# One PSUM tile of two banks made into two tiles of one bank, in a kernel of gated linear attention and a mixture of experts

## The chip, the cores and the metric

The kernel runs on one core of one Trainium2 chip. The metric is the device time of one execution in microseconds; the time of a kernel is the median of its runs. A core has a matrix engine (TensorE, PE in the rows; its weight loads are PEld), a vector engine (VectorE, DVE), a scalar engine (ScalarE, ACT), GpSimd (POOL), and SyncE (SP), which issues transfers here. The matrix engine writes into PSUM, an accumulator memory of eight banks in this program's layout, and the other engines read it from there.

## The reference

First a linear attention with a decay for each channel, over 4 batches of 8 heads, 768 steps and 48 channels a head. Its result is laid out as 3072 rows of 384 numbers. Then a mixture of 8 experts: every row is given to an expert by a greedy choice over all scores in falling order, at most 384 rows an expert, and each expert is a feed-forward network with 1024 hidden units.

```python
for t in range(S):
    state = alpha[:, :, t, :, None] * state + np.einsum('bhd,bhe->bhde', k[:, :, t], v[:, :, t])
    y[:, :, t] = np.einsum('bhd,bhde->bhe', q[:, :, t], state)
...
logits = x @ w_gate
order = np.argsort(-logits.flatten())
for idx in order:
    tok, e = (int(idx) // E, int(idx) % E)
    if assigned[tok] >= 0 or counts[e] >= cap:
        continue
    assigned[tok] = e
    counts[e] += 1
...
h = np.maximum(x[mask] @ w1[e], 0.0)
out[mask] = h @ w2[e]
```

## The kernel before

**The attention** works on 24 units: 6 chunks of 128 steps for each of the 4 batches, all 8 heads of a unit together, four pairs of two. For each unit VectorE makes running products of the decay (lines 449 and 454) and scales keys (`kh`, line 459), GpSimd scales queries (`qh`, line 464), TensorE multiplies them into scores (line 495), eight products of 128 by 128 that alternate between the two heads of a pair, and ScalarE moves the scores from PSUM to the tile `sm` (line 500), one half for each head. GpSimd masks each half (line 502), TensorE multiplies with the values (line 541), and ScalarE stores the result in `yta` (line 564).

The scores lie in the PSUM tile `s`: `[128, 2, HP, C]` with `HP` = 4 and `C` = 128, in 4-byte numbers, so two banks, one for each head of the pairs.

**The hand-over.** When the last unit is done, its router scores (lines 574 to 591) are sorted out on VectorE. Line 655 compares the keys of the last four units with the limits of the first digit, line 676 counts on TensorE, line 683 finds the threshold `gg` on VectorE, lines 901 and 902 spread it on TensorE, line 949 makes the next key `nd`, line 920 compares it with the next digit's limits, line 891 counts again, and line 895 makes the next `gg`. Further digits follow in the same manner (lines 867 to 884), then the row indices of the first expert's rows (line 1106), and GpSimd gathers these rows from `x_dram` (line 1110).

Before a row can be gathered, the attention result must lie in `x_dram` with a row's numbers next to each other. For this the result of each unit, a chunk, is turned by TensorE, four transposes a chunk in two steps of two (line 692), evicted by ScalarE into `xga` (line 696) and stored by SyncE (line 701). The first six chunks are turned in the score tile `s`, even ones in its first bank and odd ones in its second:

```python
for n in range(Y_IN_ATTENTION):
    o = sps[:, n % 2].rearrange("p a b -> p (a b)")
    xo = None
    for h in range(2):
        xo = op("PE", 0.2, shape=128, fn=lambda n=n, h=h, o=o: (turn_out(n, o, 2 * h), turn_out(n, o, 2 * h + 1)),
                r=[("yt", n)], after=[*lastw["sm", NU - 1], *([xo] if h else [])], banks=(f"S{n % 2}",), at=40.0 + n,
                take=None if h else f"s{n % 2}")
```

The other 18 are turned in the tiles `turned`, which take over the banks of `d`, `s` and `y` when the attention's pool is closed. Fills (line 291, on a tile of zeros, into `d`) stand between them on TensorE.

**The order of the work.** A planner inside the kernel (`plan`) puts the operations of all engines in an order, by durations, banks and due times that are written in the code. There are two plans, one for the attention with the six turned chunks, and one for the rest, from the routing on. The planner's own idea of the banks, the names `S0` and `S1`, keeps the two halves of the score tile apart. The order goes to a framework that adds the waits between engines. It follows tiles: an instruction waits for the earlier readers and writers of the same tile. It also has a say where the two plans meet on an engine.

Of the kernel before, what the change touches and what calls it, by code (L numbers as in the profile page):

```python
# [8 lines left out]
F32 = mybir.dt.float32  # L9
# [28 lines left out]
AF = mybir.ActivationFunctionType  # L38
# [4 lines left out]
def gla_moe_kernel(ctx, tc, q, k, v, alpha, w_gate, w12, out):  # L43
    nc = tc.nc
    C = 128
    NC = 6
    H = 8
    HP = H // 2
# [10 lines left out]
    warm = consts.tile([128, 512], BF)  # L59
# [92 lines left out]
    ps = att.enter_context(tc.tile_pool(name="ps", bufs=1, space=bass.MemoryType.PSUM))  # L152
# [24 lines left out]
    RXG = RING["xg"]  # L177

    dps = ps.tile([128, 2, 512], F32, name="d").rearrange("p a b -> p (a b)")
    sps = ps.tile([128, 2, HP, C], F32, name="s")  # L180
    yps = ps.tile([128, 2, 512], F32, name="y")
    yvs = [z[:, :, :2 * C].rearrange("p h (s t) -> p h s t", t=C) for z in (yps, dps.rearrange("p (a b) -> p a b", a=2))]
    xx = psa.tile([128, 2, 512], F32, name="xx")
# [16 lines left out]
    def op(eng, dur, fn, r=(), w=(), banks=(), at=0.0, after=(), lat=LAT, take=None, give=None, follow=(), boost=0.0,  # L200
           dma=0.0, soft=(), small=False, shape=None, ahead=0.12,
           clear=None, until=None, again=LAT):
        o = Op()
        o.small, o.shape, o.ahead, o.clear, o.until, o.again = small, shape, ahead, clear, until, again
        o.take, o.give, o.follow, o.boost, o.dma, o.soft = take, give, follow, boost, dma, soft
        o.eng, o.dur, o.fn, o.banks, o.at, o.lat = eng, dur, fn, banks, at, lat
        o.idx = len(ops)
        pre = set(after)
        for key in r:
            pre |= set(lastw[key])  # L210
            users.setdefault(key, []).append(o)
        for key in w:
            nm, ver = key
            old = (nm, ver - RING.get(nm, 1))
            pre |= set(users.get(old, ())) | set(lastw.get(old, ()))
            lastw.setdefault(key, []).append(o)
        o.pre = pre
        ops.append(o)
        return o
# [64 lines left out]
    V, G, A, P_ = nc.vector, nc.gpsimd, nc.scalar, nc.tensor  # L284
# [16 lines left out]

    def spin(n):
        for _ in range(n):
            P_.matmul(sps[:, 0].rearrange("p a b -> p (a b)"), warm[:, :128], warm, start=True, stop=True)

    def dinit():
        V.memset(dps[:, :904], 0.0)
# [2 lines left out]
    c_d = op("DVE", 1.2, dinit, w=[("dinit", 0)])  # L310
    c_pad = op("ACT", 1.9, pads, w=[("pads", 0)], banks=("Y", "KX"))
    op("PE", 4.0, lambda: spin(WARM_UP), banks=("S0",))

    def wgate():
# [120 lines left out]
    def unit(n):  # L435
        c, b = divmod(n, NBAT)
        a, sc, ga = AL[n % RING["al"]], SC[n % RING["sc"]], GA[n % RING["ga"]]
        kh, qh, kn = KH[n % RING["kh"]], QH[n % RING["qh"]], KN[n % RING["kn"]]
        sm, ms, st_ = SM[n % RING["sm"]], MS[n % RING["m"]], ST[b]
# [5 lines left out]
        for i, (lo, hi) in enumerate(parts):  # L445
            f = len(parts)
# [27 lines left out]
            if p1 > pm:  # L474
# [4 lines left out]
               r=[("q", n), ("ga", n)] + ([("kh", n)] if n in K_FIRST else []), w=[("qh", n)], at=n + 0.1)  # L479
# [11 lines left out]
        def scores():  # L491
            for p in range(HP):
                for h in range(2):
                    hs = slice(64 * h, 64 * h + 64)
                    P_.matmul(sps[:, h, p], kh[hs, p], qh[hs, p], start=True, stop=True)  # L495

        op("PE", 0.9, scores, shape=64, r=[("kh", n), ("qh", n)], w=[("S0", n), ("S1", n)], banks=("S0", "S1"),
           at=n + 0.3 - (AHEAD_S if n >= NU - 2 else 0.0))
        for h in range(2):
            op("ACT", 0.6, lambda h=h: A.activation(sm[:, h], sps[:, h], AF.Copy), r=[(f"S{h}", n)],  # L500
               w=[("sm", n)], banks=(f"S{h}",), at=n + 0.4)
            op("POOL", 0.65, lambda h=h: G.affine_select(  # L502
                sm[:, h], sm[:, h], pattern=[[0, HP], [1, C]], compare_op=OP.is_ge, fill=0.0, base=0,
                channel_multiplier=-1), r=[("sm", n)], w=[("sm", n)], at=n + 0.5)
# [12 lines left out]
        if c:  # L517
            if n in M_ACT:
                for p in range(HP):
                    op("ACT", 0.226, lambda p=p: A.activation(ms[:, p], st_[:, p], AF.Copy, scale=total[:, p:p + 1]),  # L520
                       r=[("sc", n), ("st", n - NBAT)], w=[("m", n)], at=n + 0.15)
            else:
                op("POOL", 0.5, lambda: G.tensor_tensor(ms, st_, bc(total, D), op=OP.mult),
                   r=[("sc", n), ("st", n - NBAT)], w=[("m", n)], at=n + 0.15)
# [166 lines left out]
    def turn_out(n, o, j):  # L691
        P_.transpose(o[:, C * j:C * j + KO], YT[n][:KO, j % 2, j // 2], ident[:KO, :KO])  # L692

    def y_evict(n, o):
        b, c = n % NBAT, n // NBAT
        A.activation(XG[c % RXG][:, b].rearrange("p (j g d) -> p j g d", g=2, d=D),
                     o.rearrange("p (j g d) -> p j g d", j=4, g=2)[:, :, :, :D], AF.Copy)

    def y_store(n, m=1):
        b, c = n % NBAT, n // NBAT  # L700
        nc.sync.dma_start(x_dram.rearrange("(b c p) d -> c p b d", b=NBAT, c=NC)[c][:, b:b + m],
                          XG[c % RXG][:, b:b + m])

    for n in range(NU):
        loads(n)
        unit(n)
        if n == 2:
            for i, (e, d_, f) in enumerate(rows):
                lates.append(op(e, d_, f, after=[*lates[-1:], *lastw["qh", n]], at=CONST_AT + CONST_STEP * i))
        for g, (n0, n1) in enumerate(LOGITS):  # L710
            if n1 == n + 1:
                logits(g, range(n0, n1))
        if n == GROUPS[0][1] - 1:
            first_copied = copied[-1]
# [1 line left out]
    choice(1, *GROUPS[1], copied[-1])  # L716
    ev = []
    for n in range(Y_IN_ATTENTION):
        o = sps[:, n % 2].rearrange("p a b -> p (a b)")
        xo = None  # L720
        for h in range(2):
            xo = op("PE", 0.2, shape=128, fn=lambda n=n, h=h, o=o: (turn_out(n, o, 2 * h), turn_out(n, o, 2 * h + 1)),
                    r=[("yt", n)], after=[*lastw["sm", NU - 1], *([xo] if h else [])], banks=(f"S{n % 2}",), at=40.0 + n,
                    take=None if h else f"s{n % 2}")
        ev.append(op("ACT", 0.5, lambda n=n, o=o: y_evict(n, o), after=[xo], banks=(f"S{n % 2}",), at=40.0 + n,
                     give=f"s{n % 2}"))
        op("SP", 0.1, lambda n=n: y_store(n), after=ev[-1:], at=40.0 + n)
# [674 lines left out]
```

## Time and profile before

| | us |
|---|---|
| median of 3 runs | 377.22 |
| lowest and highest run | 377.16, 380.49 |
| the profiled execution | 376.25 |
| its span, first to last instruction | 374.70 |
| TensorE busy | 354.2 |
| VectorE busy | 268.6 |
| ScalarE busy | 186.5 |
| GpSimd busy | 179.5 |

The profile records one execution, with a row for each instruction. Times in rows count from the start of the span. TensorE overlaps its products, so a busy TensorE is not one at its peak. The attention fills the span up to about 99 us, the routing of the first expert's rows goes to about 125, and the feed-forward part takes the rest, with the routing of later experts beside it.

### The profile page before, as it was taken

The page shows a single profiled execution, that of the slowest core. Times are in us where ns is not written, and L with a number is a line of the kernel's source. Part 1 is how long each engine was busy: PE and PEld are TensorE (multiplying, and loading weights), DVE is VectorE, ACT ScalarE, POOL GpSimd, SP SyncE. Part 2 cuts the span into 40 slices and gives each one's busy share as a digit, 9 for nine tenths or more (in the row PEclk, how much of TensorE's full clock was granted, in tenths as well). Part 3 has the DMA queues.
Part 4 walks back from the last instruction along what each step waited for, and adds up shares of the span by engine and source line. Part 5 has one row for each costly group of instructions (what it writes and reads, how often), then busy time and mean ns, then how long its engine had stood idle before and what let it go on. Part 6 is the DMA issues. An engine that isn't in the chain of part 4 may idle for free.

```text
span 374.7 us, 9683 instructions
## 1 busy us (share of the span) xinstructions
PE 354.2 (95%) x3716; PEld 313.3 (84%) x3716; DVE 268.6 (72%) x741; ACT 186.5 (50%) x387; POOL 179.5 (48%) x298
## 2 busy tenths in 40 slices
PE   8999999999898899999999999999999999999990
PEld 4787788887676578889989989989988999999990
DVE  7999999998747888897887987987866833131110
ACT  3587888886445371372463453444263384343120
POOL 2899999999300510524424434522731872304021
PEclk9999999999969999999999999999999999999996
DMA  7999788830138668799799699799899899985001
GB/s 251 390 400 361 243 278 261 263 107 2 44 133 318 191 235 160 218 267 213 241 269 227 212 265 218 235 244 183 276 266 193 270 359 232 286 200 118 30 21 43
DMA packets 28782, 81.71 MB, mean 218 GB/s; under 512 B 3904, under 2 KB 10304, under 8 KB 28736
## 3 DMA queue, kind: packets, MB, share of 16 engines
q0 software_dynamic: 11024, 52.70, 53.1%
q1 hardware_dynamic: 17712, 28.39, 22.4%
q8 instruction: 29, 0.48, 0.5%
q14 instruction: 17, 0.14, 0.1%
HBM read 71.64 MB, written 9.44 MB: 216 GB/s over the span
## 4 chain that ended last, share of the span: by engine, by line
PE 59%; DVE 18%; issue 10%; POOL 5%; DMA 3%; ACT 2%; POOLq 0%; DVEq 0%; ACTq 0%
PE h L1268 18%; PE y L1300 18%; PE y L541 4%; PE s L495 4%; DVE sc L449 2%; DVE ga L454 2%; DMA wset<-in_w_dram 2%; PE xt L867 2%; DVE wset L1175 2%; POOL out_dram L1320 2%; DVE kh L459 2%; PE xx L510 1%; DVE cmp L920 1%; PE turned L692 1%; PE s L692 1%
## 5 line engine op out<-in xcount | busy, mean ns | idle before, releaser
L1300 PE MATMUL y<-wset,hh 128*128 128x384 f32 x384 | 101.7, 342 | 0.0
L1268 PE MATMUL h<-xh,wset 128*128 128x384 f32 x384 | 93.4, 345 | 0.3 <-DVE hl L1283 0.3
L1281 ACT ACTIVATE hh<-h 128x384 fp32r<-128x384 f32 x64 | 31.3, 490 | 93.9 <-PE h L1268 81.8
L1300 PEld LDWEIGHTS y<-wset,hh 128*128 128x128 f32 x384 | 69.2, 188 | 1.0 <-issue 1.0
L1268 PEld LDWEIGHTS h<-xh,wset 128*128 128x128 f32 x384 | 68.1, 188 | 0.8 <-DVE hl L1283 0.6
L1300 PE MATMUL y<-wset,hl 128*128 128x384 f32 x192 | 65.9, 343 | 0.0
L1283 DVE SCALAR_TENSOR_TENSOR hl<-h,hh 128x384 fp32r<-128x384 f32 x64 | 35.3, 554 | 41.1 <-ACT hh L1281 40.6
L1193 POOL DMA_DIRECT2D wset<-in_w_dram x23 | 21.4, 932 | 63.4 <-ACT wset L1189 63.4
L1268 PE MATMUL h<-xl,wset 128*128 128x384 f32 x192 | 47.5, 345 | 0.0
L1320 POOL DMA_INDIRECT out_dram<-yo,idx x24 | 25.0, 1041 | 40.9 <-ACT yo L1311 37.0
L1189 ACT ACTIVATE wset<-wset 128x768 fp32r<-128x768 f32 x46 | 36.6, 840 | 10.8 <-DMA wset<-in_w_dram 10.7
L1110 POOL DMA_INDIRECT xr<-x_dram,idx x24 | 26.0, 1082 | 24.4 <-DVE idx L1106 8.8
L1300 PEld LDWEIGHTS y<-wset,hl 128*128 128x128 f32 x192 | 36.1, 188 | 0.1
L502 POOL TENSOR_SCALAR_AFFINE_SELECT sm<-sm 128x512 f32<-128x512 f32 x48 | 33.1, 713 | 4.2 <-ACT sm L500 3.9
L1268 PEld LDWEIGHTS h<-xl,wset 128*128 128x128 f32 x192 | 34.0, 188 | 1.0 <-issue 0.7
L464 POOL TENSOR_TENSOR qh<-qr,ga 128x512 f32<-128x512 f32 (+1 forms) x25 | 29.6, 1184 | 4.3 <-DVE sc L449 3.5
L454 DVE TENSOR_TENSOR_SCAN ga<-al,d 128x516 f32<-128x516 f32 (+1 forms) x25 | 29.6, 1183 | 1.8
L500 ACT ACTIVATE sm<-s 128x512 f32<-128x512 f32 x48 | 26.1, 595 | 8.2 <-PE s L495 7.4
L449 DVE TENSOR_TENSOR_SCAN sc<-al,d 128x516 f32<-128x516 f32 (+1 forms) x25 | 29.3, 1171 | 0.9 <-DMA al<-in_alpha_dram 0.9
L495 PE MATMUL s<-qh,kh 64*128 64x128 f32 x384 | 27.4, 282 | 0.5 <-POOL qh L464 0.2
L1163 POOL DMA_DIRECT2D raw<-in_w_dram x9 | 5.2, 580 | 46.7 <-DVE bk L1083 24.0
L541 PE MATMUL y<-sm,vr 128*48 128x128 f32 x368 | 25.2, 277 | 0.9 <-POOL sm L502 0.5
(215 smaller groups left out, 597.6 us busy)
## 6 DMA issues: line engine op xcount, KB each, us to landing
wset<-in_w_dram POOLq DMA_DIRECT2D x46, 768.0 KB
raw<-in_w_dram POOLq DMA_DIRECT2D x9, 768.0 KB
qr<-in_q_dram SPq DMA_DIRECT2D x24, 256.0 KB, 4.4
kr<-in_k_dram SPq DMA_DIRECT2D x24, 256.0 KB, 4.5
al<-in_alpha_dram SPq DMA_DIRECT2D x23, 258.5 KB, 4.4
vr<-in_v_dram SPq DMA_DIRECT2D x24, 192.0 KB, 4.4
x_dram<-xga SPq DMA_DIRECT2D x8, 384.0 KB, 2.6
x_dram<-xga SPq DMA_DIRECT2D x8, 192.0 KB, 2.5
```

What stands on the lines that cost most here:

```text
L449: V.tensor_tensor_scan(sc[:, lo + 1:hi + 1][:, ::-1], a[:, lo + 1:hi + 1][:, ::-1], dps[:, FO + lo:FO + hi][:, ::-1], 1.0, op0=OP.mult, op ...
L454: V.tensor_tensor_scan(ga[:, lo:hi], a[:, lo:hi], dps[:, lo:hi], 1.0, op0=OP.mult, op1=OP.add)
L464: (V if n in Q_DVE else G).tensor_mul(qh[:, ps_], qr[:, ps_], ga[:, lo:hi].rearrange("p (g x) -> p g x", x=C1)[:, :, 1:])
L495: P_.matmul(sps[:, h, p], kh[hs, p], qh[hs, p], start=True, stop=True)
L502: op("POOL", 0.65, lambda h=h: G.affine_select(sm[:, h], sm[:, h], pattern=[[0, HP], [1, C]], compare_op=OP.is_ge, fill=0.0, base=0, chann ...
L541: P_.matmul(yv[64 * g:64 * g + D, h, s], lhs, rhs, start=(h, g) not in fresh, stop=last and s == 1, skip_group_check=True)
L1189: pre.append(op("ACT", 0.84, lambda hs=hs: A.activation(WS[i % 2][:, 1, g][:, hs], WS[i % 2][:, 0, g][:, hs].bitcast(F32), AF.Copy, scale= ...
L1268: P_.matmul(o(), WS[i % 2][:, a, g, c0 + d * 128:c0 + (d + 1) * 128], x[:, d], start=m_ == 0 and d == 0, stop=m_ == 2 and d == DB - 1)
L1281: a_ = op("ACT", 0.49, lambda: A.activation(HHT[m], o(), AF.Relu), after=[y], r=[("hb", n_)], w=[("hh", n_)], at=at, boost=25, lat=0.1)
L1283: op("DVE", 0.474, lambda: V.scalar_tensor_tensor(HLT[m], o(), 0.0, HHT[m], op0=OP.max, op1=OP.subtract), after=[a_], r=[("hb", n_), ("hh" ...
L1300: P_.matmul(YB[b][:, :Dm], a[:, bs], w, start=q == 0 and n == 0, stop=q == FB - 1 and n == 2)
L1320: st_ = nc.gpsimd.indirect_dma_start(out=out, out_offset=bass.IndirectOffsetOnAxis(ap=IDX[i][:, b:b + 1], axis=0), in_=YO[c % 5], in_offse ...
```

## The change

The tile of two banks becomes a list of two tiles of one bank, and four places that took a half of it take one of the two. The banks are the same ones, and so are all operations.

```diff
-    sps = ps.tile([128, 2, HP, C], F32, name="s")
+    sps = [ps.tile([128, HP, C], F32, name=f"s{h}") for h in range(2)]
...
-            P_.matmul(sps[:, 0].rearrange("p a b -> p (a b)"), warm[:, :128], warm, start=True, stop=True)
+            P_.matmul(sps[0].rearrange("p a b -> p (a b)"), warm[:, :128], warm, start=True, stop=True)
...
-                    P_.matmul(sps[:, h, p], kh[hs, p], qh[hs, p], start=True, stop=True)
+                    P_.matmul(sps[h][:, p], kh[hs, p], qh[hs, p], start=True, stop=True)
...
-            op("ACT", 0.6, lambda h=h: A.activation(sm[:, h], sps[:, h], AF.Copy), r=[(f"S{h}", n)],
+            op("ACT", 0.6, lambda h=h: A.activation(sm[:, h], sps[h], AF.Copy), r=[(f"S{h}", n)],
...
-        o = sps[:, n % 2].rearrange("p a b -> p (a b)")
+        o = sps[n % 2].rearrange("p a b -> p (a b)")
```

What changes is the waits that the framework adds, and one place in the order. The rows below are instructions in the order in which they stand on an engine, with the engines or queues whose semaphores they wait for. The tile `s` is called `s_178` (first bank) and `s_179` (second bank) after the change.

On TensorE where the attention ends, chunks 0, 1 and 2 being turned, before:

```order
L692 MATMUL s<-ident,yta 128x112 x4
L585 MATMUL y<-ident,lt_175 128x128 [waits Activation_49]
L692 MATMUL s<-ident,yta 128x112 [waits Activation_49]
L692 MATMUL s<-ident,yta 128x112
L291 LDWEIGHTS warm
L291 MATMUL d<-warm 128x256
L692 MATMUL s<-ident,yta 128x112 [waits Activation_49]
L692 MATMUL s<-ident,yta 128x112
```

And after:

```order
L692 MATMUL s_178<-ident,yta 128x112 x2
L692 MATMUL s_179<-ident,yta 128x112 x2
L585 MATMUL y<-ident,lt_175 128x128 [waits Activation_49]
L692 MATMUL s_179<-ident,yta 128x112 x2
L291 LDWEIGHTS warm
L291 MATMUL d<-warm 128x256
L692 MATMUL s_178<-ident,yta 128x112 [waits Activation_49]
L692 MATMUL s_178<-ident,yta 128x112
```

The second half of chunk 1 (the row behind `L585`) waited for the eviction of chunk 0 and now waits for none; the first half of chunk 2 waited for the eviction of chunk 1 and now waits for that of chunk 0. Chunks 3, 4 and 5 are changed alike: their first halves wait for the eviction two chunks back, their second halves for none. The evictions themselves wait for the last transpose of their own chunk; before, those of chunks 0 and 2 also waited for the first half of the next chunk, and that of chunk 4 likewise.

On TensorE some 60 instructions later, where line 901 spreads the first threshold, before:

```order
L901 LDWEIGHTS one_83
L901 MATMUL xt_1881<-neg,one_83 128x1 [waits DVE_49]
L902 LDWEIGHTS one_83
L902 MATMUL xt_1881<-gg_108,one_83 128x1
L692 MATMUL s<-ident,yta 128x112 [waits Activation_49]
L692 MATMUL s<-ident,yta 128x112 x5
L692 MATMUL s<-ident,yta 128x112 [waits Activation_49]
L692 MATMUL s<-ident,yta 128x112
```

And after, from the first transpose of chunk 4 on:

```order
L692 MATMUL s_178<-ident,yta 128x112 [waits Activation_49]
L692 MATMUL s_178<-ident,yta 128x112 x3
L692 MATMUL s_179<-ident,yta 128x112 [waits Activation_49]
L692 MATMUL s_179<-ident,yta 128x112 x3
L291 LDWEIGHTS warm
L291 MATMUL d<-warm 128x256
L291 LDWEIGHTS warm
L291 MATMUL d<-warm 128x256
L901 LDWEIGHTS one_83
L901 MATMUL xt_1882<-neg,one_83 128x1 [waits DVE_49]
```

Two fills stand ahead of both pieces, and twelve transposes into the tiles `turned` behind them. The products of lines 901 and 902 stood ahead of the eight transposes of chunks 4 and 5 and of two fills, and now stand behind them. It is the only place of the whole program where the order of an engine differs.

In the attention, scores of the third unit on TensorE and their evictions on ScalarE, as a difference (- before, + after):

```order
-L495 MATMUL s<-qh_163,kh_160 128x128 [waits Activation_49,Pool_49]
-L495 MATMUL s<-qh_163,kh_160 128x128 x7
+L495 MATMUL s_178<-qh_163,kh_160 128x128 [waits Activation_49,Pool_49]
+L495 MATMUL s_179<-qh_163,kh_160 128x128 [waits Activation_49]
...
-L500 ACTIVATE sm_166<-s 128x512 [waits PE_49,Pool_49]
-L500 ACTIVATE sm_166<-s 128x512 [waits Pool_49]
+L500 ACTIVATE sm_166<-s_178 128x512 [waits PE_49,Pool_49]
+L500 ACTIVATE sm_166<-s_179 128x512 [waits PE_49,Pool_49]
```

The second head's first product waits by itself for the second eviction of the unit before, in 16 units. The second eviction waits by itself for TensorE, in all. GpSimd's mask of the first half no longer waits for TensorE in 21 units. On ScalarE there are 22 separate wait instructions more, on GpSimd 21 fewer.

## Rows read from the trace of the kernel before

**Rows 1.** Stretches (us): busy time and instructions by engine, granted clock, DMA share, GB/s.

```profile
99.20:102.70 3.50, 2.00 (x31) 1.38 (x29) 2.06 (x9) 1.47 (x3) 0.00 (x0) 0.97 0.31 112
102.70:107.00 4.30, 3.64 (x20) 2.51 (x20) 2.92 (x9) 1.42 (x3) 0.00 (x0) 0.50 0.36 122
107.00:109.50 2.50, 2.49 (x19) 2.45 (x20) 0.00 (x0) 1.04 (x3) 0.00 (x0) 0.53 0.32 115
...
111.00:119.00 8.00, 7.67 (x94) 6.33 (x92) 5.89 (x22) 5.65 (x14) 0.00 (x0) 1.00 0.75 267
...
145.00:265.00 120.00, 117.72 (x882) 108.06 (x881) 101.43 (x373) 51.03 (x87) 47.19 (x65) 1.00 0.89 228
```

**Rows 2.** Chain of work, attention: start, duration, what.

```profile
50.49 0.96 PE s L495 x16
51.45 1.60 PE y L541 x32
```

**Rows 3.** Waits of TensorE, 98 to 112: total, times, longest.

```profile
PE s L692 <- ACT xga L696: 2.1, 4, 0.6
```

**Rows 4.** Timeline of TensorE, 99 to 112: start, duration, instructions, idle before.

```profile
99.81 0.41 PE L692 MATMUL s<-ident,yta 112*128 112x112 f32 x2 [0.47 <-ACT xga L696]
...
101.05 0.65 PE L676 MATMUL xx<-o,cmp 128*128 128x8 bf16 x20
101.56 0.58 PE L692 MATMUL s<-ident,yta 112*128 112x112 f32 x4
102.72 0.64 PE L692 MATMUL s<-ident,yta 112*128 112x112 f32 x2 [0.58 <-ACT xga L696]
103.14 0.30 PE L676 MATMUL xx<-o,cmp 128*128 128x8 bf16 x4
...
107.01 2.48 PE L692 MATMUL turned<-ident,yta 112*128 112x112 f32 x12
...
110.53 1.16 PE L692 MATMUL turned<-ident,yta 112*128 112x112 f32 x10
```

**Rows 5.** Timeline of VectorE, 100 to 111.

```profile
100.58 0.69 DVE L655 TENSOR_TENSOR cmp<-m,thr 128x512 bf16<-128x512 f32 x1
...
103.48 0.17 DVE L683 TENSOR_TENSOR_SCAN gg<-xx,th 128x8 bf16<-128x8 f32 x1 [1.80 <-PE xx L676]
...
104.47 0.25 DVE L949 SCALAR_TENSOR_TENSOR nd<-dig,xt 128x24 bf16<-128x24 bf16 x1
104.76 1.90 DVE L920 TENSOR_TENSOR cmp<-nd,iota 128x1536 bf16<-128x1536 bf16 x3
110.25 0.17 DVE L895 TENSOR_TENSOR_SCAN gg<-xt,th 128x8 bf16<-128x8 f32 x1 [3.60 <-PE xt L891]
```

**Rows 6.** Chain of work, 110 to 125.

```profile
110.99 0.70 DVE cmp L920
...
113.34 0.70 DVE cmp L920
...
122.40 0.15 DVE idx L1106
...
124.40 3.14 DMA xr<-x_dram,idx
```

**Rows 7.** Lines 692 and 696: ns min/median/max, first and last start.

```profile
L692 PE MATMUL turned<-ident,yta x72: 259/259/447, 107.0 to 118.9; 112*128 112x112 f32 x72
...
L696 ACT ACTIVATE xga<-s x6: 491/491/492, 99.3 to 106.6; 128x384 f32<-128x384 f32 x6
```

**Rows 8.** Waits: lines 1110, 500 and 502 (ns); page's scores; weight load of line 541.

```profile
L1110 POOLq EVENT_SEMAPHORE  x11: 17/17/2245, 121.2 to 297.5; - x11
...
L500 ACTq EVENT_SEMAPHORE  x22: 17/17/17, 17.0 to 93.8; - x22
...
L502 POOLq EVENT_SEMAPHORE  x25: 17/17/17, 17.7 to 94.5; - x25
...
L495 PE MATMUL s<-qh,kh 64*128 64x128 f32 x384 | 27.4, 282 | 0.5 <-POOL qh L464 0.2
...
51.97 0.82 PEld L541 LDWEIGHTS y<-sm,vr 128*48 128x48 f32 x16 [0.18 <-POOL one L375]
```

## The prediction

> **What bounds the kernel now.** I read the table of stretches first, because the kernel has stages with different limits [rows 1]. In the feed-forward part TensorE is busy 117.72 of 120 us, and nothing of this change is there. In the attention part the chain of work runs on TensorE with no pause: 0.96 us of scores, then 1.60 us of products [rows 2]. Between the two lies a bad stretch of about 10 us, 99.2 to 109.5: TensorE is busy only 2.00 of 3.50 us, and then, to 109.5, its granted clock is at 0.50 and 0.53, the lower of its two levels, 1.2 GHz [rows 1]. The score tile is used here a last time, for turning six chunks of the attention result (line 692), each evicted by ScalarE (line 696).
>
> The waits name the cause: four times, 2.1 us in all, TensorE sits until an eviction of `xga` ends [rows 3]. The timeline of TensorE shows the same waits before its transposes, at 99.81 and 102.72 among others [rows 4]. Chunk n+1 has a bank of its own, yet its transposes stand behind the eviction of chunk n.
>
> Who waits for that? VectorE. Its key compare (line 655) is over at 100.58 + 0.69 = 101.27, but the four counts (line 676) that use it stand behind transposes on TensorE, at 103.14, so the threshold `gg` comes at 103.48 after 1.80 us of idleness. Later its three compares end at 104.76 + 1.90 = 106.66, and the next `gg` comes at 110.25 after 3.60 us of idleness [rows 5]: the counts of line 891 stand behind chunk transposes that run late and at the lower clock. These are the first steps of the routing, and everything behind them hangs on it: the rounds of 2.35 us (110.99 to 113.34), the row indices at 122.40, the gather at 124.40 [rows 6].
>
> **The change part by part: the hand-over.** In the order rows a half of the transposes loses its wait, and the rest waits for the eviction two chunks back. I walk TensorE through it with durations of the rows. One transpose costs (1.16 - 0.26)/9 = 0.10 us at 2.4 GHz and (2.48 - 0.45)/11 = 0.19 us at 1.2 GHz [rows 4], 0.26 and 0.45 being what the last one takes to its end [rows 7]. An eviction is 0.49 us [rows 7].
>
> Chunk 0 is now evicted when its own transposes are done, not chunk 1's first half: two transposes sooner, 99.06 to 99.55. Chunk 1 is done by 99.52 and evicted 99.57 to 100.06. Chunk 2's first half starts at 99.60 instead of 100.80 and takes 0.25 with its wait. Twenty counts take 0.50, to 100.35. Four transposes follow without a pause, chunk 2 is evicted from 100.77 to 101.26, and chunk 3's last two transposes need no wait. By 100.97 TensorE is ahead of VectorE, so the four counts start when the key compare ends, at 101.33. The threshold comes at 101.60 instead of 103.48.
>
> Next in the new order stand two fills (0.11 each), eight transposes of chunks 4 and 5 (0.80) and two more fills, and only then the product of line 901 that the threshold feeds, which stood ahead of them before. This is the part that costs: it runs at 102.65 to 102.85, though its input is there at 101.8. VectorE itself needs 104.47 - 103.48 = 0.99 us from threshold to `nd` [rows 5], so 102.60 would do; TensorE makes it 102.87. The gain at `nd` is therefore 104.47 - 102.87 = 1.60 us.
>
> The compares then end at 102.87 + (106.66 - 104.47) = 105.06. Meanwhile the twelve transposes ahead of line 891 need, at 2.4 GHz, 0.25 + 11 x 0.10, to 104.3 with the drain. So the counts no longer lag: the last four start as the compares end and are done by 105.33, and `gg` of line 895 comes at 105.35 instead of 110.25. **The gain there is 4.9 us**: 1.6 from the start of `nd`, 3.3 from TensorE having no backlog.
>
> Is it kept? Behind 110.25 VectorE and TensorE alternate on the routing rounds, with the other chunk transposes between them. The gather waits for the last store of `x_dram`: GpSimd's longest wait before a gather is 2.245 us and its first starts at 121.2, so it ends at 123.4, behind the indices of 122.40 [rows 6, 8]. Those stores come from the same transposes, in the same TensorE order, so they move as well. Weight loads are issued by an expert number that the routing finds. I find nothing started by another clock, so I carry 4.9 us to the end.
>
> **The attention part.** Three small edits repeat there. The second score product of a unit carries its own wait on ScalarE in 16 units. The second eviction waits for TensorE as well, 22 more separate waits on ScalarE. The first mask on GpSimd loses 21 waits for TensorE. Such a separate wait takes 17 ns on ScalarE's and GpSimd's queues [rows 8]: 22 x 0.017 = 0.37 us added and 21 x 0.017 = 0.36 us removed. ScalarE's is spent while the first eviction runs, so it costs nothing. GpSimd's gain is real only where GpSimd ends the chain, a few units. For TensorE's 16 waits the trace gives two bounds. Scores as a group waited 0.5 us in all, and the releaser named is GpSimd for 0.2 and never ScalarE [rows 8], so the wait is satisfied when it is reached: 0. At the head of a group with a wait the weight load sits 0.18 us [rows 8]: 16 x 0.18 = 2.9 us. But that pause also stands inside the 1.60 us of products, which are 32 at 0.05, so it is covered there [rows 2]. I take 0, and keep half of the upper end in the range.
>
> One rule of the Trainium skill speaks against the change: "TensorE: Matmul & The Clock Gate", The cost: per-tile semaphore tail, says that increments on completion serialize at about 26 ns each. The scores now signal once per bank, one increment more a unit, which by that figure is an estimate of 24 x 0.026 = 0.6 us if none is hidden. No row of this trace isolates it, and the sum above goes without it; with it the gain would be 4.3 us.
>
> **The sum.** 0 for the attention part, 4.9 us for the hand-over. The profiled execution took 376.25 us, 374.70 of it span, and would become 371.35. It stands 0.97 us below the median of the three runs, 377.22, which I take as the base: 377.22 - 4.9 = **372.3 us**.
>
> **Rivals.**
>
> *The clock falls all the same.* The pauses at 99.6 and 101.0 remain, some 0.5 us, and chunk transposes with narrow counts are not a dense load. Against it: the waits of 0.5 us that stand before the fall, which comes by 102.7, are gone, and in 111 to 119 the same mix of transposes and narrow counts runs at a clock of 1.00 [rows 1]. Price: eight transposes and twelve more at 0.19 instead of 0.10 put the counts of line 891 behind again, to 106.2 (gain 4.0), and one or two rounds of 14 transposes at 1.2 GHz add 14 x 0.09 = 1.2 us each. That leaves 1.6 to 4.0, say 2.8: 374.4 us. The Trainium skill has the mechanism on the same page, A second HAM failure mode: psum-queue depth-cycling: TensorE that idles briefly between groups as it cycles through banks swings between its two clocks. The fall from 0.97 to 0.50 in this trace agrees; the new order still cycles through two banks. Chance 0.14.
>
> *The stores take over.* The gather waits for the last store of `x_dram`, and if the stores can't come earlier, routing that is ready sooner gains nothing. Against it: behind 104 there are 18 chunks of 0.197 MB, 3.5 MB, and the stretch 111 to 119 moves 267 GB/s at a DMA share of 0.75 [rows 1], so 356 at full share: 10 us, done by 114, where I need them at 118.6. If half of the gain is lost there: 374.8 us. Chance 0.05.
>
> *Only the waits of line 692 go.* If TensorE keeps its backlog before line 891 for a reason that I don't see, such as waits of the turned tiles on the tiles they replace, only the 1.6 us at `nd` stay: 375.6 us. Against it: the first of these tiles waits for a fill that ends at 102.8, and the later ones for evictions over by 103.2. Chance 0.05.
>
> *Slower.* The wait on the second score product breaks the side-by-side run of the two heads: sixteen passes take 0.96 us, 0.06 apart, though each is in flight for 272 ns [rows 2, 8]. The attention chain has no slack on TensorE, so all of it would count. It decides from 4.9/24 = 0.20 us a unit. At 0.35 us, a third of a group, it is 8.4 - 4.9 = 3.5 us slower: 380.7 us. Against it: the wait stands on the second product alone, at a semaphore long reached. Chance 0.03.
>
> **How the numbers follow.** The forecast has 0.73. Its own spread is 0.6 us of GpSimd waits to the good and 1.4 us of score waits to the bad, 371.7 to 373.7. The range takes in the clock rival at its middle and a little of run-to-run difference below: 370.8 to 374.6. What a measurement of this kernel can tell from no change is about 1%, 3.8 us: faster than 373.4 us is most of the forecast and a little of the clock rival, 0.77; within 1% is the rest of these and the two that lose the gain, 0.20; slower by more 0.03.
>
> **What would show it.** Right: no wait of TensorE for `xga` over 0.2 us between 98 and 107; the granted clock at 1.00 through 99 to 111; `gg` of line 683 near 101.6, `nd` near 102.9, `gg` of line 895 near 105.4; the gather near 119.5. Attention ending within 0.5 us of where it did. Wrong: a lower clock behind 102; VectorE idle for over 1 us before line 895; a gather that waits long after the last index; scores that take over 1 us as a group in the chain.

## Result and the profile after

The changed kernel takes 372.78 us (median of 4 runs, 372.38 to 373.59), the kernel before 377.71 us beside it (4 runs). The ratio is 0.9853 with a 95% interval of 0.9811 to 0.9895: 4.9 us, 1.5%, faster. The forecast was 372.3 us with a gain of 4.9. A second set of runs (chip C below) gave 372.07 against 377.75 us, ratio 0.9847 (0.9806 to 0.9888). Ratios, and the table of executions further down, leave out the disturbed executions (over 1.5% longer than the quickest of the same kernel); all other medians are over all executions.

The waits of TensorE between 98 and 112 of the changed kernel, line by line with total, times and longest, where four for `xga` stood before [rows 3]:

```profile
PE xx L676 <- DVE cmp L655: 0.2, 1, 0.2
```

The products now wait once, 0.2 us, and for VectorE. For an eviction only a weight load still waits, 0.24 us to 99.17, while the product ahead of it is running. The same stretches as in [rows 1], busy time and instructions of PE, PEld, DVE, ACT and POOL, then granted clock, DMA share and GB/s:

```profile
99.20:102.70 3.50, 3.28 (x49) 2.95 (x50) 2.81 (x14) 2.16 (x5) 0.00 (x0) 1.00 0.61 218
102.70:107.00 4.30, 4.23 (x64) 3.40 (x63) 3.35 (x7) 2.52 (x6) 0.00 (x0) 1.00 0.56 196
107.00:109.50 2.50, 2.37 (x33) 1.93 (x31) 1.72 (x6) 1.36 (x3) 0.00 (x0) 1.00 0.87 312
111.00:119.00 8.00, 6.99 (x70) 4.87 (x69) 6.73 (x35) 2.73 (x7) 0.60 (x1) 1.00 0.89 294
...
145.00:265.00 120.00, 117.09 (x895) 106.96 (x894) 100.48 (x364) 52.67 (x89) 49.69 (x67) 1.00 0.88 233
```

The granted clock is 1.00 in all of these stretches, and TensorE runs 64 products from 102.70 to 107.00 where it ran 20. The timeline of the changed kernel over the hand-over, all engines, answers to [rows 4, 5]:

```profile
96.87 0.60 ACT L564 ACTIVATE yta<-d 128x512 f32<-128x512 f32 x1 [1.32 <-PE d L541]
...
99.17 0.41 PE L692 MATMUL s<-ident,yta 112*128 112x112 f32 x2
...
99.42 0.65 PE L676 MATMUL xx<-o,cmp 128*128 128x8 bf16 x20
...
100.14 0.69 DVE L655 TENSOR_TENSOR cmp<-m,thr 128x512 bf16<-128x512 f32 x1
...
100.89 0.26 PE L676 MATMUL xx<-o,cmp 128*128 128x8 bf16 x4 [0.19 <-DVE cmp L655]
...
101.18 0.17 DVE L683 TENSOR_TENSOR_SCAN gg<-xx,th 128x8 bf16<-128x8 f32 x1
...
102.21 0.17 PE L901 MATMUL xt<-neg,one 128*128 128x1 bf16 x1
...
102.43 1.37 PE L692 MATMUL turned<-ident,yta 112*128 112x112 f32 x12
102.45 0.25 DVE L949 SCALAR_TENSOR_TENSOR nd<-dig,xt 128x24 bf16<-128x24 bf16 x1 [0.38 <-PE xt L902]
102.73 1.90 DVE L920 TENSOR_TENSOR cmp<-nd,iota 128x1536 bf16<-128x1536 bf16 x3
...
104.98 0.17 DVE L895 TENSOR_TENSOR_SCAN gg<-xt,th 128x8 bf16<-128x8 f32 x1 [0.35 <-PE xt L891]
```

VectorE waits 0.35 us before line 895 instead of 3.60, and the twelve transposes take 1.37 us instead of 2.48. Line 564's last row (the end of the attention) stood at 97.31 in the profiled execution of before:

```profile
97.31 0.60 ACT L564 ACTIVATE yta<-d 128x512 f32<-128x512 f32 x1 [1.31 <-PE d L541]
```

So this execution of the changed kernel came out of the attention 0.44 us sooner. The chain of work behind it, where [rows 6] show before:

```profile
105.72 0.70 DVE cmp L920
...
108.06 0.70 DVE cmp L920
...
117.13 0.15 DVE idx L1106
...
119.27 0.75 POOL xr L1110
```

The gather starts at 119.27 instead of 124.40, 5.13 us sooner.

### The profile page after: what moved, and what is told of

It is laid out like the page before. It is cut to its first block, busy times and chain, and to the rows that moved or that the text cites. A ratio compares the mean times of both kernels' runs of the same rounds, so it can differ in the third digit from the quotient of the medians.

```text
span 371.0 us, 9684 instructions
## 1 busy us (share of the span) xinstructions
PE 351.1 (95%) x3716; PEld 311.4 (84%) x3716; DVE 268.4 (72%) x741; ACT 185.7 (50%) x387; POOL 178.6 (48%) x298
## 4 chain that ended last, share of the span: by engine, by line
PE 54%; DVE 22%; issue 11%; POOL 5%; DMA 5%; ACT 2%; POOLq 0%; DVEq 0%; ACTq 0%
PE h L1268 18%; PE y L1300 17%; PE y L541 4%; PE s L495 4%; DVE sc L449 3%; DVE ga L454 3%; DVE kh L459 3%; PE xt L867 2%; DVE wset L1175 2%; DMA wset<-in_w_dram 2%; POOL out_dram L1320 2%; DMA raw<-in_w_dram 1%; DVE hl L1283 1%; DVE cmp L920 1%; PE xx L510 1%
## 5 line engine op out<-in xcount | busy, mean ns | idle before, releaser
L502 POOL TENSOR_SCALAR_AFFINE_SELECT sm<-sm 128x512 f32<-128x512 f32 x48 | 32.1, 692 | 3.3 <-ACT sm L500 3.0
L495 PEld LDWEIGHTS s<-qh,kh 64*128 64x128 f32 x384 | 23.8, 189 | 2.1 <-POOL qh L464 1.4
```

Source lines behind the costliest of these rows:

```text
L495: P_.matmul(sps[h][:, p], kh[hs, p], qh[hs, p], start=True, stop=True)
L502: op("POOL", 0.65, lambda h=h: G.affine_select(sm[:, h], sm[:, h], pattern=[[0, HP], [1, C]], compare_op=OP.is_ge, fill=0.0, base=0, chann ...
```

## Experiments

The first four kernels ran on one chip (A in the table below), the next two on a second (B), the last four on a third (C), each time beside the kernel before.

**The hand-over without the attention's split.** The kernel before, its score tile undivided, with odd chunks turned in another tile:

```diff
-        o = sps[:, n % 2].rearrange("p a b -> p (a b)")
+        o = dps[:, :512] if n % 2 else sps[:, 0].rearrange("p a b -> p (a b)")
...
-        P_.matmul(dps[:, 512:768], warm[:, :128], warm[:, :2 * C], start=True, stop=True)
+        P_.matmul(yps[:, 0, 2 * C:], warm[:, :128], warm[:, :2 * C], start=True, stop=True)
```

> The kernel before with its undivided score tile, but the odd ones of the six turned chunks go into the first bank of the tile d, and the fills, which used d, go into y. Attention waits are those of before; the hand-over has two tiles. Theory (the gain is made where the chunks are turned): the threshold of line 895 near 105.5 us, granted clock 1.00 throughout, time about 4.9 us below before, ratio 0.987. Rival (the gain is in the attention, where each head's scores are evicted for themselves): ratio 1.00.

Measured: 373.94 us, ratio 0.9874 (0.9836 to 0.9911) against a before of 379.35 on this chip. Its timeline reads like that of the changed kernel:

```profile
102.43 0.25 DVE L949 SCALAR_TENSOR_TENSOR nd<-dig,xt 128x24 bf16<-128x24 bf16 x1 [0.37 <-PE xt L902]
...
104.96 0.17 DVE L895 TENSOR_TENSOR_SCAN gg<-xt,th 128x8 bf16<-128x8 f32 x1 [0.35 <-PE xt L891]
```

All of the gain is there, and the attention, with before's waits, ends at 96.85 (line 564), no later than with the split, 96.87.

**The split without its effect on the hand-over.** The changed kernel, with all chunks in the two halves of one undivided tile (and the fills moved to `y` as above):

```diff
-        o = sps[n % 2].rearrange("p a b -> p (a b)")
+        o = dps[:, 512 * (n % 2):512 * (n % 2) + 512]
```

> The changed kernel with its two score tiles, but the six chunks are turned in the two halves of the undivided tile d, and the fills go into y. Attention waits are those of after; the hand-over waits as before. Theory: TensorE waits some 2 us for the evictions of line 696 again, the clock falls, the threshold of line 895 comes at 109.5 to 110.5 us, ratio 0.998 to 1.001. Rival (attention): ratio 0.987.

Measured: 379.48 us, ratio 1.0011 (0.9967 to 1.0055). The four waits are back, and with them the low clock, in the same views:

```profile
PE d L692 <- ACT xga L696: 2.1, 4, 0.6
```

```profile
102.70:106.20 3.50, 2.90 (x19) 2.29 (x20) 2.71 (x9) 0.98 (x2) 0.00 (x0) 0.55 0.34 118
106.20:109.50 3.30, 3.15 (x26) 2.63 (x25) 0.21 (x1) 1.56 (x4) 0.00 (x0) 0.50 0.34 121
109.50:113.00 3.50, 3.50 (x47) 3.39 (x45) 1.45 (x4) 1.80 (x4) 0.00 (x0) 0.50 0.45 164
113.00:116.50 3.50, 3.50 (x32) 3.43 (x31) 1.93 (x7) 1.57 (x5) 0.00 (x0) 0.50 0.62 225
```

What the split does in the attention is worth nothing that these runs can tell, for good or ill.

**The waits kept, the clock held.** The kernel before, with four fills on TensorE ahead of each of the four transposes that wait:

```diff
+            before_ = [xo] if h else ev[-1:] and [turned_half]
+            if (h and n % 2) or (not h and n == 2):
+                for _ in range(4):
+                    before_ = [op("PE", 0.0, fill_d, shape=128, banks=("D0", "D1"), at=40.0 + n, boost=30.0,
+                                  after=[*before_, *lastw["sm", NU - 1], *lastw["yt", NU - 1]])]
...
```

> The kernel before with four more fills ahead of each of four transposes that wait for an eviction, so that TensorE is busy in those waits and the waits themselves stay. It tells the price of the lower clock from that of the waits. Theory: the granted clock stays at 1.00; chunk transposes at 0.10 instead of 0.19 us put the threshold of line 895 near 107.5, 2.7 us sooner than before, ratio 0.993; what is left to after, 2.2 us, is the waits. Rival (the clock costs nothing, only the waits count): ratio 1.00. Rival (the clock is all): ratio 0.987.

Measured: 376.57 us, ratio 0.9956 (0.9918 to 0.9993). The four transposes are delayed as before (their weight loads still wait four times, 1.4 us in all, for an eviction), but TensorE has products to run meanwhile, and the clock stays at 1.00 to 109.5. VectorE's two thresholds and `nd` (six lines are added, so lines 949 and 895 are 955 and 901 here):

```profile
102.79 0.17 DVE L683 TENSOR_TENSOR_SCAN gg<-xx,th 128x8 bf16<-128x8 f32 x1 [1.13 <-PE xx L676]
103.79 0.25 DVE L955 SCALAR_TENSOR_TENSOR nd<-dig,xt 128x24 bf16<-128x24 bf16 x1
...
107.44 0.17 DVE L901 TENSOR_TENSOR_SCAN gg<-xt,th 128x8 bf16<-128x8 f32 x1 [1.47 <-PE xt L897]
```

The second threshold lies 2.8 us ahead of before's 110.25 and 2.5 us behind the changed kernel's 104.98: about half of the gain is the clock's, half the waits' own. (The attention ended 0.46 us sooner than in before here, line 564 at 96.85, so the clock's half is 2.3 to 2.8 us by this profile.) On one chip the medians say the same: 379.35 before, 376.57 here (2.8 us), 373.94 with two tiles (2.6 us more). From the end of the attention to the gather it took 124.40 - 97.31 = 27.1 us before, 121.36 - 96.85 = 24.5 here and 119.27 - 96.87 = 22.4 in the changed kernel: 2.6 for the clock, 2.1 for the waits.

**No fills.** The changed kernel with `for _ in range(80)` at the operations of the fills behind the attention made `range(0)`.

> The changed kernel without the fills of line 291. Theory: two banks keep TensorE busy enough by themselves, the clock stays at 1.00, line 949 starts 0.3 us sooner than in after as VectorE's own chain decides there, ratio to before 0.986. Rival (the fills are what holds the clock in after): the clock falls behind 101 us, the threshold of line 895 comes 1 us or more later than in after, ratio 0.990 to 0.995.

Measured: 372.76 us, ratio 0.9851 (0.9773 to 0.9929). `nd` is at 102.27, the second threshold at 104.80, the gather at 119.09, all 0.2 us sooner, and the clock stays at 1.00. The four fills that stand ahead of line 901 cost 0.2 us at this place, too little for the time to show, and they aren't what holds the clock. Without them TensorE pauses for 0.68 us ahead of the last four counts of line 676 (at 100.96), and no fall follows.

**Four chunks in the score tiles.** The changed kernel with `Y_IN_ATTENTION = 4` instead of 6.

> The changed kernel with four chunks turned in the score tiles instead of six, so the product of line 901 no longer stands behind the eight transposes of chunks 4 and 5, which go to the turned tiles. The prediction's step that priced this move at 0.27 us: nd at 102.1 to 102.2 instead of 102.45, and gg of line 895 0.2 to 0.3 us earlier than 104.98; the time stays within 0.5 us of the changed kernel. Rival, that these transposes are needed early because the chunks' stores set the gather: gg earlier, but the gather not, or later than 119.27. If the pile of transposes in front of line 891 grows instead (twenty instead of twelve, some 2.2 us at 0.10 each), its counts lag behind the compares, gg of line 895 is not earlier.

Measured: 376.15 us, ratio 0.9911 (0.9863 to 0.9958). The small step came as expected (`nd` 102.30, second threshold 104.83, though the key compare of line 655 starts 0.12 us later than in the changed kernel). The time did not get shorter: by the ratios 0.9911 - 0.985 = 0.6%, 2.3 us of the gain are lost. How much of this is real is not clear, as the intervals of the two ratios overlap and the six executions that the ratio takes lie between 370.91 and 376.31 us. In the profiled one TensorE, whose first twelve transposes into the turned tiles start 0.9 us sooner, now pauses 0.7 us behind them, and the clock falls with no wait of its products for an eviction ahead of that. TensorE's only wait over 0.2 us, and the stretches:

```profile
PE xt L891 <- DVE cmp L920: 0.7, 1, 0.7
```

```profile
102.70:106.20 3.50, 2.80 (x42) 2.04 (x39) 2.84 (x7) 1.50 (x4) 0.00 (x0) 0.99 0.38 136
106.20:109.50 3.30, 3.25 (x28) 3.11 (x28) 2.06 (x7) 1.77 (x5) 0.00 (x0) 0.50 0.67 238
109.50:113.00 3.50, 3.50 (x41) 3.40 (x39) 1.67 (x5) 1.92 (x5) 0.00 (x0) 0.50 0.62 225
```

The gather comes at 121.14, 1.9 us later than in the changed kernel, though the second threshold was there sooner. These are the numbers of the rival in the expectation, but not its mechanism. The routing rounds have slowed before any store is waited for: from `nd` to `nd` it is 110.95 - 107.83 = 3.12 us at the low clock, against 110.13 - 107.78 = 2.35 in the changed kernel. The last index is there at 118.52 + 0.32 = 118.84 instead of 117.28. Yet this execution took 372.16 us, no longer than the profiled one of the changed kernel (372.59): behind the gather it needed 370.6 - 121.1 = 249.5 us, the changed kernel 371.0 - 119.3 = 251.7. So the fall of the clock and the later gather are shown, and that this one fall makes the kernel slower is not. Over the six executions a lower mean clock goes with a longer time (371.19 and 370.91 us at 0.993 and 0.988, 376.31 and 375.99 at 0.983 and 0.981), but no profile shows where the clock was low in the long ones.

**Three tiles.** The changed kernel without the fills, and with a third tile, the first bank of `d`:

```diff
-        o = sps[n % 2].rearrange("p a b -> p (a b)")
+        k = n % 3
+        o = dps[:, :512] if k == 2 else sps[k].rearrange("p a b -> p (a b)")
+        bank = ("S0", "S1", "D0")[k]
...
```

> The changed kernel with a third tile for the chunks (the first bank of d), and without the fills behind the attention. No transpose then waits for an eviction at all that is not long over. Theory, that two tiles already take every wait that mattered: gg of line 683 stays at 101.2, since its counts wait for the compare of line 655 on VectorE, and the time is that of the changed kernel, 372.8, within 0.5 us. Rival, that the pauses which remain before chunk 2 (some 0.3 us twice) still cost: gg of line 683 and everything behind it 0.3 to 0.6 us earlier, 372.2 to 372.5 us. If the clock needed the transposes spread out, a granted clock under 1.00 behind 101 and a time of 374 or more.

Measured: 372.76 us (4 runs), ratio 0.9885 (0.9818 to 0.9953). The expectation was wrong in one place: a wait is left, of the first transpose into the turned tiles for the last eviction, 0.55 us to 102.15. `nd` was at 101.80, but the second threshold at 105.57. Two executions have a mean clock of 0.992, the others 0.986 and 0.982; the last one is the profiled one, and the fall comes at the end of this wait:

```profile
99.20:102.70 3.50, 2.46 (x30) 2.16 (x27) 3.10 (x13) 1.76 (x5) 0.00 (x0) 0.92 0.69 239
102.70:106.20 3.50, 3.50 (x42) 3.39 (x41) 1.58 (x5) 1.47 (x3) 0.00 (x0) 0.50 0.54 193
```

So I asked how often the clock falls in each kernel, with four more kernels on a third chip.

**The changed kernel and three tiles a second time, and three tiles with fills.** Of the last two, the first puts four fills (into `y`) into TensorE's pause ahead of the last four counts of line 676, the second three more ahead of line 901 (the last four lines are the second kernel's alone):

```diff
+            pre = [xo] if h else turned_half[-1:]
+            if n == 4 and not h:
+                for _ in range(4):
+                    pre = [op("PE", 0.0, fill_d, shape=128, banks=("Y",), at=40.0 + n, boost=30.0, after=pre)]
+            elif not h:
+                pre = []
...
-    for _ in range(0):
-        op("PE", 0.115, fill_d, shape=128, banks=("D0", "D1"), at=60.0, until=ev[-1], after=lastw["yt", NU - 1])
+    for _ in range(80):
+        op("PE", 0.115, fill_d, shape=128, banks=("Y",), at=60.0, until=ev[-1], after=lastw["yt", NU - 1])
```

> The changed kernel a second time, to see in how many executions its granted clock falls behind the attention, since the two kernels with other tiles (four chunks; three tiles) had falls without a wait for an eviction. Theory that the removed waits alone decide: nearly all executions at a mean clock of 0.989 or more, as in the four so far, median 372.8 within 1 us. Rival, that the fall is a matter of chance in every version and four executions were lucky: a third or more below 0.988, and the median above 374.

> The kernel with three tiles and no fills a second time, on the same chip as the changed kernel. If the pauses that it leaves on TensorE (0.5 us ahead of the last four counts, 0.6 us ahead of the first transposes into the turned tiles) put the clock at risk, a good part of the executions lies below 0.988, and those are some 2 to 3 us longer than the others; the others are 0.5 to 1 us quicker than the changed kernel.

> Three tiles, and four fills in the pause of TensorE ahead of the last four counts of line 676 (0.11 us each, in the second part of y's first bank). If TensorE's pauses decide on the clock, fewer executions with a fall than three tiles without fills; nd at 101.8 as there, gg of line 895 near 104.3 where the clock stays, the gather near 118.6, and the median 0.5 us or more below the changed kernel. If the fills make no difference: as many falls as without them.

> The same with three more fills ahead of the product of line 901. Theory: the pause ahead of the turned tiles is shorter by 0.3 us, so the clock is safer still, but the product runs later: nd up to 0.3 us later than 101.8. Rival: no difference to four fills beyond 0.3 us.

Measured, in this order: 372.07, 372.61, 371.98 and 372.65 us, ratios 0.9847 (0.9806 to 0.9888), 0.986 (0.9821 to 0.99), 0.984 (0.98 to 0.988) and 0.9847 (0.9805 to 0.9889). On this chip the three kernels with three tiles have a mean clock of 0.989 or more in 16 of 18 executions (five of six without fills), so that two of four were low on chip B did not repeat, and what the fills do for the clock can't be told. With four fills the pause ahead of the counts is gone; `nd` is at 102.30, the second threshold at 104.83 and the gather at 119.12, each 0.5 us later than expected, as is the end of the attention (96.83, where the first profile of three tiles had 96.32). With seven, 0.2 us of the wait ahead of the turned tiles are left, and `nd` is at 102.37. The median with four fills was expected 0.5 us or more below that of the changed kernel, and is 0.1 below. None of the three is faster than the changed kernel by an amount that these runs can separate. The second profile of three tiles has the same two waits of TensorE as the first:

```profile
PE turned L692 <- ACT xga L696: 0.6, 1, 0.6
PE xx L676 <- DVE cmp L655: 0.5, 1, 0.5
```

but its clock stays at 1.00 and its transposes run at their pace, where the first one's took 2.50 us. The timelines of the first and then of the second:

```profile
102.15 2.50 PE L692 MATMUL turned<-ident,yta 112*128 112x112 f32 x12 [0.55 <-ACT xga L696]
```

```profile
103.67 1.37 PE L692 MATMUL turned<-ident,yta 112*128 112x112 f32 x12 [0.55 <-ACT xga L696]
```

Its attention ended at 97.84, the first one's at 96.32 (line 564). From there to the gather it took 120.12 - 97.84 = 22.3 us, the first 120.69 - 96.32 = 24.4 us. It is the same program, so **2.1 us is what one fall of the clock cost here**. (The two ran on different chips, but without a fall the same way took the changed kernel 22.4 us in its first profile and 22.5 on chip C.) The second profile of the changed kernel has its gather at 119.18, its clock at 1.00.

The executions, by the mean granted clock of each:

| kernel | chip | executions | clock 0.989 or more | their median, us | median of the others, us |
|---|---|---|---|---|---|
| before | A | 21 | 4 | 376.68 | 379.35 |
| waits kept, fills in them | A | 10 | 9 | 376.43 | 378.82 |
| two tiles, attention undivided | A | 10 | 9 | 373.89 | 376.62 |
| one tile for the chunks | A | 10 | 2 | 376.43 | 379.75 |
| changed kernel, no fills | A | 4 | 4 | 372.76 | |
| before | B | 13 | 1 | 375.20 | 377.47 |
| four chunks | B | 6 | 1 | 371.19 | 373.81 |
| three tiles | B | 4 | 2 | 371.49 | 373.57 |
| before | C | 11 | 1 | 376.11 | 377.96 |
| changed kernel | C | 6 | 6 | 372.08 | |
| three tiles | C | 6 | 5 | 372.54 | 373.48 |
| three tiles, four fills | C | 6 | 6 | 371.98 | |
| three tiles, seven fills | C | 6 | 5 | 372.58 | 373.83 |

The four executions of the changed kernel that belong to the result are also all at 0.989 or more. The mean clock doesn't say where it was low, so the table is read with the profiles, not in their place. It says two things. The kernel before is at 0.989 or more in 6 of 45 executions, and on chip A these were 2.7 us shorter (379.35 to 376.68), about what the fills in the waits gained (2.8). From there to the two tiles it is another 2.8 us (376.68 to 373.89) at mean clocks alike, which fits the waits' own part.

## Why the prediction was right, and where its reason was too narrow

**The waits.** Right: 2.1 us of waits in four became none. The four counts start 0.06 us after the compare's end (100.14 + 0.69 = 100.83, then 100.89), as the walk through TensorE said. The threshold came 0.42 us ahead of the forecast 101.60, and the attention had ended 0.44 us sooner: the step itself was exact.

**The new place of line 901.** Right, and its size too: from the threshold to `nd` it took 102.45 - 101.18 = 1.27 us, forecast 102.87 - 101.60 = 1.27. Without the fills ahead of it, it is 102.27 - 101.26 = 1.01, and without the transposes (four chunks) 102.30 - 101.29 = 1.01, so either way it is back at VectorE's own pace, before's 0.99. So the step did cost the 0.27 that was assumed. Undoing it with four chunks brought no gain: the clock fell in the profile, and the ratio is 0.9911.

**TensorE's backlog before line 891.** Right: from `nd` to the second threshold 2.53 us, forecast 2.48. The whole gain there is 110.25 - 104.98 = 5.27, of which 0.44 is the earlier end of the attention; 4.83 stand against the 4.9 of the sum.

**Carried to the end.** Right up to the gather, 5.13 - 0.44 = 4.7 us. GpSimd's wait before it now starts at 115.9 and lasts 2.395 us, to 118.3, 1.0 us behind the last index (117.28); before it was 121.2 + 2.245 = 123.4 against 122.55. The view doesn't name what this wait is for. That it is the last store is read from its end, 2.7 us behind the issue of the last store at 115.6 (before 3.0 us, at 120.4). The stores then still come last, by the same margin, and moved along, which was the answer given to that rival. In GpSimd's queue (POOLq):

```profile
L1110 POOLq EVENT_SEMAPHORE  x11: 17/17/2395, 115.9 to 294.0; - x11
```

The profiled executions differ by only 376.25 - 372.59 = 3.7 us at the end. The one of before was quick for its kernel, as the forecast had said of its 0.97 us below the median; the medians differ by 4.9 and, on chip C, 5.7. Behind the gather the changed kernel's profiled execution took 1.4 us longer than that of before (251.7 against 374.7 - 124.4 = 250.3). Over all profiles this part varies from 249.5 to 253.0 us, and no run shows what sets it; that the gain reaches the end rests on the medians, not on one pair of profiles.

**The attention at 0.** Right as far as can be told. The earlier end of 0.44 us is not the split's: the kernel with before's waits there ended at 96.85, the one with the split but without the new hand-over at 97.30. One program, three tiles, ended at 96.32 in one execution and at 97.84 in another (on two chips), so a term of some tenths can't be read here. The Trainium skill's rule in "TensorE: Matmul & The Clock Gate", The cost: per-tile semaphore tail, by whose figure the estimate was 0.6 us of loss, finds no support: the two-tile kernel has no second signal in the attention, and its end at 96.85 is that of the changed kernel within 0.02; a cost of some tenths isn't excluded, with the differences above. One term of the forecast's spread doesn't follow from its working: it takes 0.6 us of GpSimd waits to the good, where the working has 21 x 0.017 = 0.36. No run shows either, and the result doesn't hang on it.

**The clock.** The forecast that it stays was right: both profiles of the changed kernel show 1.00 over the hand-over, and all ten executions have a mean of 0.989 or more. The reason was too narrow: the four waits of line 692 are one way to lose it, and the forecast argued as if it were kept once they are gone. With four chunks it falls at 106.2 with none of these waits, with three tiles at 102.2 in one execution behind a wait that another one has too. What the rival "the clock falls all the same" describes thus happened, though in kernels that differ by a few instructions, not in the changed one. The rival left 1.6 to 4.0 us of the gain of 4.9, 2.8 in the middle, which prices a fall at 0.9 to 3.3 us, 2.1 in the middle. Measured are 2.1 (three tiles with the fall and without), 2.6 and 2.8 (fills in the waits) and 2.7 (executions of before on chip A). The sum itself doesn't say that its 4.9 holds two parts of like size, 2.1 to 2.8 of clock and 2.1 to 2.8 of waits, nor that the first depends on something that varies between executions of one program. The Trainium skill has a clock that swings between its two levels in "TensorE: Matmul & The Clock Gate", A second HAM failure mode: psum-queue depth-cycling, as a matter of brief idling between groups. The kernel with fills in the waits agrees: same delay, products in place of the pauses, clock at 1.00 in its profile. Idling alone doesn't decide, though: without fills the changed kernel pauses for 0.68 us and keeps 1.00, and with four chunks 0.7 us stand 2.6 us ahead of a fall.

**Open:** what decides it. The busy times of TensorE alone don't tell: with seven fills the profile has a fall of 3.4 us at 124.2, outside the hand-over, behind a stretch that looks just like the same one in the changed kernel, where there is none. The stretches with seven fills, and then of the changed kernel:

```profile
121.00:124.20 3.20, 1.70 (x21) 1.28 (x21) 2.50 (x7) 2.25 (x4) 2.90 (x3) 1.00 0.39 113
124.20:127.60 3.40, 3.40 (x14) 2.10 (x14) 0.87 (x4) 1.24 (x4) 1.38 (x3) 0.50 0.86 282
```

```profile
121.00:124.20 3.20, 1.70 (x21) 1.19 (x20) 2.90 (x8) 1.96 (x4) 2.90 (x4) 1.00 0.46 127
124.20:127.60 3.40, 3.17 (x21) 2.18 (x21) 1.55 (x4) 2.04 (x5) 0.96 (x2) 1.00 0.97 314
```

## What to carry to other kernels

A framework that tracks waits by tiles sees one tile where a plan sees two banks; where two halves of a tile are filled and emptied in turns, make them two tiles, and look for the gain at the place where the turns are on the path (here a hand-over of 6 us), not where the halves are used side by side. When waits of half a microsecond stand in a stretch of light work on TensorE, price them twice, once as delay and once as clock: here 2.1 us of waits cost 2.1 to 2.8 us as delay and as much again as clock. Since the second part varies between executions of one program, compare the mean clocks of all runs, not one profile; and before small work is moved off such a stretch to save 0.2 us, look whether a pause opens in its place, as it did with four chunks instead of six. There the clock fell and nothing was gained; that the pause made it fall is not shown.

## What was not expected of the hardware

Whether the clock falls is not settled by the program alone: the kernel before had a mean clock of 0.989 or more in 6 of 45 executions, and three tiles fell at 102.2 in one profiled execution and not in another on a second chip, with the same waits. The stretches at 0.50 that the profiles show are 102.5 to 109.3 in before, 106.2 to 113.0 with four chunks, 102.2 to 109.0 in the first profile of three tiles, 124.2 to 127.6 with seven fills and 103.0 to 116.7 with one tile for the chunks. In the last of these the work from the second threshold to the gather took 126.11 - 110.30 = 15.8 us, against 124.40 - 110.25 = 14.2 in before and 119.27 - 104.98 = 14.3 in the changed kernel: before had already paid for its fall by then.
